# Sliding-window attention and token MLP on one core: values by four column tiles, keys in halves of 32, and a new order

## The chip, the cores and the metric

The kernel runs as one program on 1 core of one Trainium2 chip. The metric is the device time of one launch in microseconds (us); the median of several runs is compared. A core has a matrix engine (TensorE, PE in the profile, with its weight loads as PEld), a vector engine (VectorE, DVE), a scalar engine (ScalarE, ACT), a general engine (GpSimd, POOL) and a sync engine (SyncE, SP), whose queue issues nearly all DMAs here. Each engine takes its own list of instructions in order and waits on semaphores for the others. PE writes to PSUM; the others bring results from there to SBUF.

## The reference

```python
# x: [1, 2048, 512]; 32 heads of 16; window of 256 keys, causal
mod = (silu(c) @ w_mod)            # six vectors of 512: sa, ca, ga, sb, cb, gb
h = layernorm(x) * (1 + ca) + sa
q, k, v = split(h @ wqkv)          # wqkv: [512, 1536]
scores = q @ k.T * 16 ** -0.5      # kept where 0 <= query - key < 256
o = softmax(scores) @ v
x = x + ga * (o @ wo)
h = layernorm(x) * (1 + cb) + sb
u = gelu(einsum('bsd,sf->bdf', layernorm(h), w1) + b1)   # over tokens, f = 1792
y = einsum('bdf,fs->bds', u, w2) + b2
out = x + gb * y.transpose
```

All tensors are bf16.

## The kernel before

**Stages.** The 2048 tokens are cut into four row groups G of 512, each of two halves H of 256 queries. For each G the kernel normalizes x, transposes it (on PE for the first group, by DMA transposes into `h1T` for the others), and makes q, k and v with `wqkv` (`proj0` for the first group, `proj` for the rest). Then come the attention, `wo` and the next norms (`post`), and the token MLP: partial sums over finished token tiles (`partials`, pieces p), the rest of the first matmul (`tail`, pieces u), and last the output matmuls `py`, written out after the ordered part.

**Operations and their order.** All but the last stage is written as 1165 small operations (`Op`), each with an engine or a choice of engines, a cost and the operations it depends on. The list ORDER, written out in full, says in which order they are issued; CHOSEN says which engine takes each of the 177 operations that have a choice. `run_schedule` walks ORDER and emits each operation on its engine, so ORDER is the order in every engine's queue, SP's among them. The names used below are those of the operations: S (scores of a chunk, PE), EA and EB (their exponentials, ACT), M (mask, DVE), AV (values and sums, PE), ln and rz (logarithm of the sums and its exponential, ACT), OT (product, DVE), k, q, v (projections, PE), ke, qe, ve (their copies out of PSUM), kk (keys split by parity of the head), vo and vp (values placed), xn, h1T, hb, n2 (norm pieces), xt (DMA transpose), p and u (MLP, PE), wo.

**Attention in chunks.** A chunk is 512 score columns for four pairs of heads, in which four row tiles of 32 rows (two heads of 16) work at once. A column stands for one query, and the 128 partitions of a chunk hold 64 keys of each of two heads: `KT` holds, for every block of 64 keys, the keys once with the odd and once with the even heads zeroed, `[P, 8, 2, KB]`. There are 75 chunks. EA covers three of the four PSUM banks of a chunk (1536 columns), EB the fourth (512). Masks come from `maskt`, `[P, 3, KB]`, built once on POOL from triangles in `tmpm`. AV multiplies the exponentials with `VT` on four column tiles of 32, and with `ones_bd` for the sums.

**Values.** `VT[r]` has for each block of 64 keys 128 partitions, the first 64 for one head of a pair, the last 64 for the other; each half is nonzero in 16 of 32 columns. For the first group `v` makes both halves directly: two column tiles of 64, each with the 256 columns of wqkv of one parity, then a copy `vb`, and two copies multiplied with `mask_half` (all 128 partitions, 512 columns each). For the other groups `v` is a plain matmul with tokens on the partitions (four pieces of 512 columns, or sixteen in column tiles of 32). The result `vb` then has one half of the keys on the wrong partitions: `vx` swaps them by two DMAs into `vs`, `vo` copies the half that lies right, `vp` the swapped one (two copies of 64 partitions each). VT[1] is zeroed by a memset on POOL (`z`), VT[2] by two DMAs (`z2`), since these copies write the nonzero places only.

**Column tiles for dense work.** `run_schedule` marks dense PE pieces (k, q, v, wo, p) that stand near an AV in a run between two score chunks as `tiled`: `mm` then issues four matmuls of 32 output rows each instead of one of 128, so that the shape of the tiles on PE need not change.

**PSUM.** Three banks, `od`, are shared by all projections, AV, wo and p; an operation takes the bank that comes free first.

Of the kernel before, what the change touches and what calls it, by code (L numbers as in the profile page):

```python
# [13 lines left out]
P = 128  # L14
S = 2048
# [8 lines left out]
KB = 64  # L24
HQ = 4 * KB
# [91 lines left out]
]  # L117
CHOSEN = {
    "ACT": [
        47, 48, 50, 51, 74, 82, 1062,  # L120
    ],
    "DVE": [
# [5 lines left out]
    ],  # L128
    "POOL": [
# [86 lines left out]
def kernel(  # L216
# [31 lines left out]
    class Ordered:  # L248
        def __init__(self, engine):
            self.engine = engine  # L250

        def __getattr__(self, name):
            call = getattr(self.engine, name)

            def wrapped(*args, **kwargs):
                ins = call(*args, **kwargs)  # L256
                if pinned[0]:
                    tc.keep_in_program_order(ins)
# [1176 lines left out]
```

## Time and profile before

| what | us |
|---|---|
| median of 3 runs | 254.74 |
| lowest, highest | 253.11, 255.09 |
| span of the profiled execution | 252.3 |
| PE busy | 235.3 |
| DVE busy | 205.4 |
| ACT busy | 179.5 |
| POOL busy | 126.3 |

The span runs from the first to the last instruction of one profiled execution; the runs' times take in what lies around it. Busy time is the time in which an engine had at least one instruction running; since matmuls are pipelined and their ends are modelled, a busy PE is not PE at its peak. In the rows of single instructions the columns are start in us, duration in us, engine, line, operation, tile written and tiles read, shapes and count, and in brackets the idle time of the engine just before and what ended it. In the rows of groups they are count, busy us, mean ns of one, and idle us before them. Nearly every instruction has line 256, a helper through which all of them are issued, so groups are told apart by their tiles.

### The profile page before, as it was taken

What the parts mean: (1) busy time and instruction counts of PE and PEld (TensorE: products, weight loads), DVE (VectorE), ACT (ScalarE), POOL (GpSimd) and SP (SyncE); (2) the same over time, 40 slices, a digit from 0 to 9 for tenths busy, and PEclk for the clock granted to TensorE, in tenths of its full rate; (3) what the DMA queues carried; (4) which work ended last, traced back from release to release, by engine and by line L of the source; (5) the groups of instructions that cost most, each with busy time, mean ns of one, the idle gap of its engine ahead of it and who ended that gap; (6) DMA issues with size and microseconds to landing.
All of it is one profiled execution on the core that took longest, in us unless ns stands there. A gap on an engine that the chain in (4) does not pass through costs nothing.

```text
span 252.3 us, 9189 instructions
## 1 busy us (share of the span) xinstructions
PE 235.3 (93%) x3949; PEld 126.0 (50%) x3949; DVE 205.4 (81%) x408; ACT 179.5 (71%) x254; POOL 126.3 (50%) x228
## 2 busy tenths in 40 slices
PE   7988888899987889999999999999999999999995
PEld 2656644445554544555546454556444444444443
DVE  5499998989989998999897999999978764444443
ACT  4699998999999999999999999997147510000000
POOL 8268968795899989845886348173000000000000
PEclk9999999999999999999999999999999999999999
DMA  6999364356055200003401536314999201111111
GB/s 200 323 351 294 48 47 86 44 70 187 3 74 112 53 23 3 4 3 104 131 3 45 155 82 189 105 44 113 343 388 386 108 22 43 44 52 52 42 44 42
DMA packets 42625, 28.13 MB, mean 111 GB/s; under 512 B 12376, under 2 KB 38488, under 8 KB 42584
## 3 DMA queue, kind: packets, MB, share of 16 engines
q1 hardware_dynamic: 42576, 27.54, 39.4%
q8 instruction: 31, 0.51, 0.9%
q14 instruction: 10, 0.08, 0.1%
q10 hardware_dynamic: 8, 0.00, 0.0%
HBM read 22.03 MB, written 2.10 MB: 96 GB/s over the span
## 4 chain that ended last, share of the span: by engine, by line
PE 52%; ACT 24%; DVE 7%; DMA 5%; issue 5%; POOL 4%; SPq 1%; POOLq 0%; DVEq 0%
ACT et L256 20%; PE py L256 19%; PE pu L256 16%; PE po L256 5%; PE pss L256 5%; ACT lz L256 3%; PE pa L256 3%; DMA x<-in_A_x_dram 2%; DVE et L256 2%; DMA h1T<-xn 2%; DMA wmod<-in_w_mod_dram 1%; POOL h1T L256 1%; PE pq L256 1%; DVE st L256 1%; PE pk L256 1%
## 5 line engine op out<-in xcount | busy, mean ns | idle before, releaser
L256 ACT ACTIVATE et<-pss 128x1536 bf16<-128x1536 f32 x75 | 110.7, 1476 | 2.8 <-PE psb L256 2.3
L256 PE MATMUL py<-guT,w2r 128*128 128x512 bf16 (+2 forms) x238 | 48.7, 366 | 0.0
L256 ACT ACTIVATE et<-psb 128x512 bf16<-128x512 f32 x75 | 46.9, 626 | 0.0
L256 DVE TENSOR_TENSOR et<-et,maskt 128x1024 bf16<-128x1024 bf16 (+2 forms) x79 | 46.4, 603 | 0.1
L256 PE MATMUL pu<-hb,w1s 128*32 128x512 bf16 (+1 forms) x302 | 39.0, 380 | 0.2 <-DVE QT L256 0.2
L256 PEld LDWEIGHTS <-w2r 128*128 128x128 bf16 x238 | 22.8, 98 | 26.1 <-issue 0.3
L256 PE MATMUL pss<-QT,KT 32*128 32x64 bf16 (+3 forms) x720 | 29.9, 230 | 6.2 <-ACT et L256 3.5
L256 PE MATMUL po<-et,VT 128*32 128x64 bf16 (+3 forms) x960 | 32.2, 234 | 1.3 <-DVE kb L256 0.6
L256 PE MATMUL po<-et,ones_bd 128*32 128x256 bf16 (+3 forms) x624 | 31.7, 268 | 0.0
L256 PEld LDWEIGHTS <-KT 32*128 32x128 bf16 x960 | 17.1, 92 | 28.5 <-issue 24.6
L256 DVE TENSOR_TENSOR otile<-py,xr 128x512 bf16<-128x512 f32 (+2 forms) x17 | 11.2, 660 | 24.4 <-PE py L256 24.2
L256 POOL TENSOR_SCALAR KT<-kb,mask_par 128x512 bf16<-128x512 bf16 (+1 forms) x36 | 25.0, 707 | 11.4 <-DVE kb L256 11.1
L256 PE MATMUL psb<-QT,KT 32*128 32x64 bf16 (+3 forms) x240 | 29.3, 231 | 0.0
L256 PEld LDWEIGHTS <-VT 128*32 128x32 bf16 x960 | 20.8, 96 | 13.2 <-issue 4.7
L256 PE MATMUL pk<-h1T,wqkv 128*32 128x512 bf16 (+4 forms) x228 | 21.1, 340 | 2.4 <-DVE OT L256 1.0
L256 DVE BATCH_NORM_STATS2 st<-x 128x6 f32<-128x512 bf16 x32 | 21.5, 680 | 2.1 <-DMA x<-in_A_x_dram 2.1
L256 PEld LDWEIGHTS <-wqkv 128*32 128x32 bf16 (+1 forms) x350 | 15.3, 96 | 12.7 <-issue 4.7
L256 PEld LDWEIGHTS <-w1s 128*32 128x32 bf16 (+1 forms) x302 | 14.1, 97 | 15.0 <-issue 1.5
L256 PE MATMUL pv<-wqkv,h1T 128*32 128x512 bf16 (+2 forms) x202 | 17.1, 348 | 1.3 <-DVE OT L256 0.7
L256 PE MATMUL pu<-hb,w1r 128*128 128x512 bf16 (+1 forms) x96 | 17.9, 380 | 0.0
L256 PE MATMUL pa<-wod,OT 128*32 128x512 bf16 (+1 forms) x136 | 17.2, 381 | 0.0
L256 PEld LDWEIGHTS <-ones_bd 128*32 128x32 bf16 x624 | 15.8, 97 | 0.1
(109 smaller groups left out, 350.1 us busy)
## 6 DMA issues: line engine op xcount, KB each, us to landing
w2r<-in_B_w_dram SPq DMA_DIRECT2D x14, 512.0 KB, 10.2
w1s<-in_B_w_dram SPq DMA_DIRECT2D x19, 256.0 KB, 4.0
w1r<-in_B_w_dram SPq DMA_DIRECT2D x9, 256.0 KB, 4.3
x<-in_A_x_dram SPq DMA_DIRECT2D x16, 128.0 KB, 5.2
wmod<-in_w_mod_dram SPq DMA_DIRECT2D x4, 512.0 KB, 7.8
out_dram<-otile SPq DMA_DIRECT2D x15, 128.0 KB, 1.7
wmod<-in_w_mod_dram SPq DMA_DIRECT2D x4, 256.0 KB, 3.9
wqkv<-in_A_wqkv_dram SPq DMA_DIRECT2D x4, 256.0 KB, 5.7
```

The costliest lines, as they stand in the source:

```text
L256: ins = call(*args, **kwargs)
```

## The change

Five things change; the number of operations and the names stay.

1. The values of all groups are made like this, for each half n of a token tile, with four column tiles of 32 partitions (32 tokens each, one parity of the heads each). They then lie on the right partitions, and are placed by two masked copies over all 128 partitions, as in the first group before. The swaps and both zero fills go; their operations stay in the list as empty ones.
2. The partitions of a chunk change their order: 32 keys of one head, the same 32 of the other, then the next 32 of each. `KT`, `mask_half`, `ones_bd` and `maskt` follow.
3. Pieces in units of 32 columns allow new shapes of chunks (`NEAR_MIXED`, `FAR_MIXED`, one chunk of 256 columns for both), used for the first MIXED pairs; MIXED is 0. `maskt` has ten parts instead of three, for these shapes too.
4. `v` counts as a neighbour that makes dense pieces `tiled`, the first group's too, which had a class of its own before. `vb` has three buffers instead of two.
5. ORDER and CHOSEN are new lists; each instruction also gets an explicit dependency, without a semaphore, on the one before it on its engine.

```diff
+QB = 32
...
-        sums = [n for n, o in enumerate(run) if o.name == "AV"]
+        sums = [n for n, o in enumerate(run) if o.name == "AV" or o.name == "v"]
...
-NEAR = [(-1, 0, 4, 0), (0, 0, 4, 256)]
+MIXED = 0
+NEAR = [(-1, 0, 8, 0), (0, 0, 8, 256)]
...
+                    if self.last is not None:
+                        tc.add_manual_dep(
+                            ins.ins, self.last, mybir.DependencyInfo(mybir.DependencyClass.NoSync, mybir.DependencyReason.DATA),
+                            reason="order",
+                        )
+                    self.last = ins.ins.name
...
-    KT = [[kvpool.tile([P, 8, 2, KB], BF, name=f"KT{r}_{g}") for g in range(ND)] for r in range(3)]
+    KT = [[kvpool.tile([P, 8, 2, 2, QB], BF, name=f"KT{r}_{g}") for g in range(ND)] for r in range(3)]
...
-        1: [op("z", "POOL", 3.45, lambda e: po.memset(VT[1][:], 0.0), ready=2.0, pos=-22.0)],
+        1: [op("z", "POOL", 0.05, lambda e: None, pos=-22.0)],
...
+    def values(dst, h1T, tb, n):
+        wv = wqkv[:, :, 2 * D : 3 * D].rearrange("p j (a two d) -> p j two a d", two=2, d=DH)
+        for dc in range(ND):
+            for r in range(4):
+                tok = tb * P + n * KB + r // 2 * QB
+                te.matmul(
+                    dst[QB * r : QB * (r + 1), n, :].rearrange("p (a d) -> p a d", d=DH),
+                    lhsT=h1T[:, dc, tok : tok + QB], rhs=wv[:, dc, r % 2, :, :],
+                    start=(dc == 0), stop=(dc == ND - 1), tile_position=(0, QB * r), skip_group_check=True,
+                )
+
+    def place(eng, dst, src, tb, half):
+        eng.tensor_scalar(
+            out=dst[:, 2 * tb : 2 * tb + 2, :, half * DH : (half + 1) * DH],
+            in0=src[:].rearrange("p i (a d) -> p i a d", d=DH),
+            scalar1=mask_half[:, half : half + 1], scalar2=0.0, op0=ALU.mult, op1=ALU.add,
+        )
...
-            zeros[2].append(op("z2", "SP", 2.6, lambda e, n=n: dma.dma_start(
-                out=VT[2][:, 4 * n : 4 * n + 4, :, :].rearrange("p b a d -> p b (a d)"),
-                in_=nothing[:].unsqueeze(1).to_broadcast([P, 4, D]),
-            ), deps=zeros[2] + k_done[0, 1][-1:], pos=14.0 + n, ready=30.0, extra=1.0))
+            zeros[2].append(op("z2", "SP", 0.0, lambda e: None, deps=zeros[2] + k_done[0, 1][-1:], pos=14.0 + n, extra=-2.0))
...
-            def e_vx(e):
-                vs = box["vs", tb] = work.tile([P, 256], BF, name="vs", tag=vs_tag, bufs=1)
-                dma.dma_start(out=vs[0:KB, :], in_=box["vb", tb][KB:P, 0, :])
-                dma.dma_start(out=vs[KB:P, :], in_=box["vb", tb][0:KB, 1, :])
...
-            vx = op("vx", "SP", 1.05, e_vx, deps=[ve_op], pos=pos, extra=0.1)
-            own = op("vo", {"POOL": 0.78, "DVE": 0.45}, 0.78, lambda e: e_vp(e, True), deps=[ve_op] + war + zeros[r3], pos=pos)
-            b = op("vp", {"POOL": 0.78, "DVE": 0.45}, 0.78, lambda e: e_vp(e, False), deps=[vx] + war + zeros[r3], pos=pos)
+            vx = op("vx", "SP", 0.0, lambda e: None, deps=[ve_op], pos=pos, extra=-2.0)
+            placed = [
+                op(("vo", "vp")[half], {"POOL": 0.78, "DVE": 0.45}, 0.78,
+                   lambda e, half=half: place(ENGINE[e], VT[r3], box["vb", tb], tb, half), deps=[ve_op] + war, pos=pos)
+                for half in range(2)
+            ]
```

In CHOSEN the changes by name, engine before and after, are: m2 four from DVE to POOL and four back; n2 four to POOL, two to DVE; hb four to POOL, one to DVE; xn three to POOL, one to DVE; kk three to DVE, one to POOL; vo two each way; vp two to DVE; h1T two from DVE to POOL, one from POOL to DVE, one from ACT to DVE; ke one from ACT to DVE; ve one from DVE to ACT.

More of the change, by code (lines that the diff above doesn't have):

```diff
@@ L250, in __init__ @@
             self.engine = engine
+            self.last = None
         def __getattr__(self, name):
@@ L300 @@
     wod = const.tile([P, ND, D], BF, name="wod")
-    maskt = const.tile([P, 3, KB], BF, name="maskt")
+    maskt = const.tile([P, 10, QB], BF, name="maskt")
     ones_bd = const.tile([P, 2 * DH], BF, name="ones_bd")
     nc.gpsimd.memset(ones_bd[:], 0.0)
-    nc.gpsimd.memset(ones_bd[0:KB, 0:DH], ZSCALE)
-    nc.gpsimd.memset(ones_bd[KB:P, DH : 2 * DH], ZSCALE)
+    for r in range(4):
+        nc.gpsimd.memset(ones_bd[QB * r : QB * (r + 1), r % 2 * DH : (r % 2 + 1) * DH], ZSCALE)
     nothing = const.tile([P, D], BF, name="nothing")
@@ L380, in emit_masks @@
     def emit_masks():
-        tmpm = modw.tile([P, 2, 2, KB], BF, name="tmpm")
+        tmpm = modw.tile([P, 3, 2, KB], BF, name="tmpm")
+        masks = maskt[:].rearrange("p m k -> p (m k)")
         po.memset(tmpm[:], 1.0)
-        for half in range(2):
+        for n in range(3):
             po.affine_select(
-                out=tmpm[:, half, 0, :], in_=tmpm[:, half, 0, :], pattern=[[-1, KB]],
-                compare_op=ALU.is_ge, fill=0.0, base=-1 - KB * half, channel_multiplier=1,
+                out=tmpm[:, n, 0, :], in_=tmpm[:, n, 0, :], pattern=[[-1, KB]],
+                compare_op=ALU.is_ge, fill=0.0, base=-1 - QB * n, channel_multiplier=1,
             )
             po.affine_select(
-                out=tmpm[:, half, 1, :], in_=tmpm[:, half, 1, :], pattern=[[1, KB]],
-                compare_op=ALU.is_ge, fill=0.0, base=KB * half, channel_multiplier=-1,
-            )
-        for half in range(2):
-            rows = slice(KB * half, KB * half + KB)
-            for i in range(3):
-                po.tensor_copy(out=maskt[rows, i, :], in_=tmpm[rows, half, min(i, 1), :])
+                out=tmpm[:, n, 1, :], in_=tmpm[:, n, 1, :], pattern=[[1, KB]],
+                compare_op=ALU.is_ge, fill=0.0, base=QB * n, channel_multiplier=-1,
+            )
+        for r, n in enumerate((0, 1, 1, 2)):
+            rows = slice(QB * r, QB * (r + 1))
+            both = tmpm[rows, n, :, :].rearrange("p s k -> p (s k)")
+            parts = both.rearrange("p (n k) -> p n k", k=QB)
+            po.tensor_copy(out=masks[rows, 0:128], in_=both)
+            po.tensor_copy(out=masks[rows, 128:192].rearrange("p (n k) -> p n k", k=QB), in_=parts[:, 0:4:3, :])
+            for to, part in ((192, 1), (256, 2)):
+                po.tensor_copy(
+                    out=masks[rows, to : to + KB].rearrange("p (n k) -> p n k", k=QB),
+                    in_=parts[:, part : part + 1, :].to_broadcast([QB, 2, QB]),
+                )
     ops = []
@@ L812, in e_v @@
                     box["v", tb] = bank([P, 2, 256], F32, "pv")
-                wv = wqkv[:, :, 2 * D : 3 * D].rearrange("p j (a two d) -> p j two a d", two=2, d=DH)
-                tok = slice(tb * P + n * KB, tb * P + (n + 1) * KB)
-                for dc in range(ND):
-                    for par in range(2):
-                        te.matmul(
-                            box["v", tb][KB * par : KB * (par + 1), n, :].rearrange("p (a d) -> p a d", d=DH),
-                            lhsT=h1T[:, dc, tok], rhs=wv[:, dc, par, :, :],
-                            start=(dc == 0), stop=(dc == ND - 1), tile_position=(0, KB * par),
-                        )
+                values(box["v", tb], h1T, tb, n)
             def e_ve(e):
@@ L974, in e_v @@
                 if n == 0:
-                    box["v", tb] = bank([P, D], F32, "pv")
-                for dc in (2 * n, 2 * n + 1):
-                    mm(
-                        box["v", tb][:], h1T[:, dc, tb * P : (tb + 1) * P], wqkv[:, dc, 2 * D : 3 * D],
-                        (dc == 0), (dc == ND - 1),
-                    )
-            def e_ve(e):
-                vb = box["vb", tb] = work.tile([P, 2, 256], BF, name="vb", tag=vb_tag, bufs=1)
-                copy(
-                    e, vb[:].rearrange("p two (a d) -> p a two d", d=DH),
-                    box["v", tb][:].rearrange("p (a two d) -> p a two d", two=2, d=DH),
-                )
-            def e_vx(e):
-                vs = box["vs", tb] = work.tile([P, 256], BF, name="vs", tag=vs_tag, bufs=1)
-                dma.dma_start(out=vs[0:KB, :], in_=box["vb", tb][KB:P, 0, :])
-                dma.dma_start(out=vs[KB:P, :], in_=box["vb", tb][0:KB, 1, :])
-            def e_vp(e, own):
-                for half in range(2):
-                    rows = slice(KB * half, KB * half + KB)
-                    block, src = (half, box["vb", tb][rows, half, :]) if own else (1 - half, box["vs", tb][rows, :])
-                    ENGINE[e].tensor_copy(
-                        out=VT[r3][rows, 2 * tb + block, :, half * DH : (half + 1) * DH],
-                        in_=src.rearrange("p (a d) -> p a d", d=DH),
-                    )
-            vb_tag, vs_tag = turn("vb"), turn("vs")
+                    box["v", tb] = bank([P, 2, 256], F32, "pv")
+                values(box["v", tb], h1T, tb, n)
+            def e_ve(e):
+                box["vb", tb] = work.tile([P, 2, 256], BF, name="vb", tag=vb_tag, bufs=1)
+                copy(e, box["vb", tb][:], box["v", tb][:])
+            vb_tag = turn("vb", 3)
             war = [av_ops[G - 2, g] for g in range(ND)] if G >= 2 else []
@@ L1168, in e_s, with score @@
                 box["sb", i] = ps_b.tile([P, D], F32, name="psb")
-                for unit, kb, qs, nq, col in pieces:
-                    g8, Hh = unit["g8"], unit["H"]
-                    block = 4 * Hh + kb
-                    q0 = (Hh % 2) * HQ + KB * qs
+                def score(unit, kb, q, width, col, side=None):
+                    block = 4 * unit["H"] + kb
+                    own = KT[block // 8 % 3][unit["g8"]]
+                    q += (unit["H"] % 2) * HQ
+                    part = slice(0, P) if side is None else slice(KB * side, KB * (side + 1))
                     for j in range(4):
                         rows = slice(32 * j, 32 * j + 32)
-                        dst = box["sa"][:, j, col : col + KB * nq] if j < 3 else box["sb", i][:, col : col + KB * nq]
+                        dst = box["sa"][part, j, col : col + width] if j < 3 else box["sb", i][part, col : col + width]
                         te.matmul(
-                            dst, lhsT=KT[block // 8 % 3][g8][rows, block % 8, :, :],
-                            rhs=QT[unit["G"] % 2][g8][rows, q0 : q0 + KB * nq],
-                            start=True, stop=True, tile_position=(32 * j, 0), skip_group_check=True,
-                        )
+                            dst, lhsT=own[rows, block % 8, :, :, :] if side is None else own[rows, block % 8, side, :, :],
+                            rhs=QT[unit["G"] % 2][unit["g8"]][rows, q : q + width],
+                            start=True, stop=True, tile_position=(32 * j, part.start), skip_group_check=True,
+                        )
+                for unit, kb, qs, nq, col in pieces:
+                    if kb is not None:
+                        score(unit, kb, QB * qs, QB * nq, col)
+                    else:
+                        for qb in range(4):
+                            for side in range(2):
+                                score(unit, qb - 4 * side, KB * qb + QB * side, QB, col + QB * qb, side)
             def e_ea(e, i=i, lo=lo, hi=hi):
```

112 lines of the change are left out of this document (69 added, 43 removed), and 123 rows, old and new, of tables (CHOSEN, ORDER).

## The prediction

> **What bounds the kernel now.** I read the page first, then the engines' busy time in six stretches, then the chain of waits, then single rows. The page's totals and its slices come first:
>
> ```profile
> span 252.3 us, 9189 instructions
> PE 235.3 (93%) x3949; PEld 126.0 (50%) x3949; DVE 205.4 (81%) x408; ACT 179.5 (71%) x254; POOL 126.3 (50%) x228
> PE   7988888899987889999999999999999999999995
> ACT  4699998999999999999999999997147510000000
> ```
>
> By shares PE is the bound and ACT is at 71%. The slices say otherwise: ACT is full from the third slice to the twenty-eighth and then nearly idle. So I cut the span where the second exponential starts (14.58), where PE becomes full (115), just behind the last score chunk (171) and at the first output matmul (200.94). Columns: PE, weight loads, DVE, ACT, POOL.
>
> ```profile
> 14.58:115.00 100.42, 89.74 (x2126) 51.91 (x2128) 94.99 (x189) 98.92 (x134) 82.78 (x140) 1.00 0.38 81
> 115.00:171.00 56.00, 55.32 (x1228) 30.13 (x1224) 51.97 (x96) 55.40 (x74) 33.42 (x59) 1.00 0.35 97
> 171.00:200.94 29.94, 29.94 (x257) 14.57 (x246) 26.19 (x61) 15.06 (x30) 1.73 (x2) 1.00 0.80 281
> 200.94:252.30 51.36, 48.55 (x239) 22.57 (x236) 24.09 (x39) 1.70 (x3) 0.00 (x0) 1.00 0.12 42
> ```
>
> From 14.58 to 171 ACT is busy 154.3 of 156.4 us: the exponentials set the pace, and DVE, at 147, has little room either. PE has 10.7 us of room up to 115 and none after. Behind the last score chunk PE alone counts, without a gap:
>
> ```profile
> 169.87 0.26 PE L256 MATMUL pss<-QT,KT 32*128 32x192 bf16 x3
> 178.50 22.45 PE pu L256 x104
> 203.78 45.75 PE py L256 x225
> ```
>
> So the time is: start of the exponentials, plus ACT's work and ACT's stalls up to the last score chunk, plus the PE work left behind it. Only the middle term has slack, and little. The group row sums ACT's stalls, and three single rows show what one is:
>
> ```profile
> L256 ACT ACTIVATE et<-pss 128x1536 bf16<-128x1536 f32 x75 | 110.7, 1476 | 2.8 <-PE psb L256 2.3
> 11.22 1.45 ACT L256 ACTIVATE et<-pss 128x1536 bf16<-128x1536 f32 x1 [0.73 <-PE psb L256]
> 40.47 1.45 ACT L256 ACTIVATE et<-pss 128x1536 bf16<-128x1536 f32 x1 [0.64 <-PE psb L256]
> 83.05 1.45 ACT L256 ACTIVATE et<-pss 128x1536 bf16<-128x1536 f32 x1 [0.42 <-PE psb L256]
> ```
>
> In each the score matmuls came late from PE. All 75 exponentials together stood 2.8 us, 0.73 of it before the first one; the other 2.1 us is all that a better order can take out of the middle term.
>
> **The change, part by part.** *The work behind the last score chunk.* I walked both ORDER lists to the last S entry. Behind it the old list has 56 u, 4 p, 4 wo and 7 AV, the new one the same with 6 AV. The AV that moves ahead of it (two times 512 columns, at 22.45 / 104 = 0.216 us each: 0.43) lands where PE is full as well, so I count nothing. MIXED is 0, so no chunk takes the new mixed shapes: 75 chunks with the old column counts, and ACT's exponentials stay as they are.
>
> *Values on PE.* A token tile was 4 matmuls of 512 columns on the whole array (or 16 in column tiles), in the first group 16 of 256 columns on two tiles; it becomes 32 of 256 columns on four. The trace has that count and shape for keys:
>
> ```profile
> 28.69 1.06 PE L256 MATMUL pk<-h1T,wqkv 128*32 128x256 bf16 x32 [0.39 <-DVE bc_ga L256]
> 14.47 1.06 PE L256 MATMUL pv<-wqkv,h1T 128*64 128x256 bf16 x16
> L256 PE MATMUL pv<-wqkv,h1T 128*128 128x512 bf16 x18 | 4.7, 380 | 0.6 <-DVE vb L256 0.6
> ```
>
> 32 such matmuls took 1.06 us, as the two-tile form did, against 4.7 / 4.5 = 1.04 us for a tile of the whole-array form. Cost of the new form: nothing. Walking the lists, the tile shape on PE changes 153 times instead of 158: nothing I can price above a few tenths, and up to 115 under ACT's cover.
>
> *Placing the values.* Four copies of half the partitions become two masked copies of all; the zero fills go.
>
> ```profile
> L256 POOL COPY VT<-vs 64x256 bf16<-64x256 bf16 x24 | 10.8, 452 | 3.9 <-DMA vs<-vb 3.0
> L256 POOL COPY VT<-vb 64x256 bf16<-64x256 bf16 x20 | 10.2, 511 | 3.5 <-DVE vb L256 2.9
> L256 DVE COPY VT<-vb 64x256 bf16<-64x256 bf16 x4 | 0.9, 216 | 0.0
> L256 POOL TENSOR_SCALAR VT<-vb,mask_half 128x512 bf16<-128x512 bf16 x8 | 5.8, 731 | 1.3 <-DVE vb L256 1.3
> L256 POOL MEMSET VT<- 128x4096 bf16 x1 | 3.5, 3517 | 0.1
> L256 DVE TENSOR_SCALAR KT<-kb,mask_par 128x512 bf16<-128x512 bf16 x2 | 1.0, 526 | 0.0
> ```
>
> By CHOSEN 20 of the 24 new copies are on POOL: 20 x 0.731 = 14.6 against 10.8 + 10.2 + 3.5 = 24.5 us, so POOL gains 9.9. Four are on DVE, priced at the like key copy: 4 x 0.526 = 2.1 against 0.9, so DVE pays 1.2.
>
> [...]
>
> *Masks.* POOL builds them from six selects instead of four and sixteen copies instead of six:
>
> ```profile
> L256 POOL COPY maskt<-tmpm 64x64 bf16<-64x64 bf16 x6 | 1.2, 234 | 0.0
> L256 POOL TENSOR_SCALAR_AFFINE_SELECT tmpm<-tmpm 128x64 bf16<-128x64 bf16 x4 | 0.9, 268 | 0.1
> 13.15 3.03 POOL L256 TENSOR_SCALAR KT<-kb,mask_par 128x256 bf16<-128x256 bf16 x6 [5.19 <-DVE kb L256]
> 11.75 0.69 DVE L256 BATCH_NORM_STATS2 st<-x 128x6 f32<-128x512 bf16 x1 [1.02 <-DMA x<-in_A_x_dram]
> ```
>
> 10 x 0.234 + 2 x 0.268 = 2.9 us more, less the 3.5 of the memset ahead of them: they end no later, and POOL then stood idle 5.19 us anyway. Without that cover the first key copies would be late.
>
> The last row also fixes the start. The second chunk's keys wait on DVE for statistics of an x tile that lands at 11.75, and both lists have those statistics ahead of the key copy. So the second exponential stays near 14.58, although one h1T piece goes from ACT to DVE before it.
>
> *ACT's own list.* One key copy leaves it, one value copy (512 columns) enters behind the third exponential:
>
> ```profile
> 14.26 0.37 ACT L256 ACTIVATE kb<-pk 128x256 bf16<-128x256 f32 x1
> 14.58 1.45 ACT L256 ACTIVATE et<-pss 128x1536 bf16<-128x1536 f32 x1
> 15.93 0.59 ACT L256 ACTIVATE et<-psb 128x512 bf16<-128x512 f32 x1
> ```
>
> The 0.37 lay before 14.58 and saves nothing. The entering copy, at the 0.59 of a 512-column piece, which overlaps its neighbour by 0.1, costs +0.5 us, with every exponential queued behind it.
>
> *SP's queue.* 24 swaps and two fills go from it:
>
> ```profile
> vs<-vb SPq DMA_DIRECT2D x24, 32.0 KB, 1.9
> VT<-nothing SPq DMA_DIRECT2D x2, 512.0 KB, 4.7
> SPq L256 <- DVE vb L256: 55.3, 6, 23.4
> ```
>
> SP stood 55.3 us waiting for vb, with transposes and w1 loads queued behind. That makes inputs early, not PE late: in no row above did PE or ACT wait for a swap or a load, so I take nothing; the bound on the other side is ACT's 2 us.
>
> *The order.* The second h1T piece of group 1 goes from POOL to DVE, so the two run side by side:
>
> ```profile
> 39.70 0.40 PE L256 MATMUL pk<-h1T,wqkv 128*32 128x512 bf16 x4 [0.70 <-POOL h1T L256]
> L256 POOL TENSOR_SCALAR h1T<-h1T,modFM 128x512 bf16<-128x512 bf16 x8 | 7.2, 907 | 2.4 <-DMA h1T<-xn 2.3
> L256 DVE TENSOR_SCALAR h1T<-h1T,modFM 128x512 bf16<-128x512 bf16 x4 | 1.5, 426 | 0.0
> ```
>
> The pair ends up to 2 x 0.907 us earlier, which takes away the 0.70 wait and with it the 0.64 stall of ACT at 40.47. Next late there are the DVE copies of k and q. Net of all moves POOL takes three hb, two n2, two xn and one h1T, and DVE two key splits:
>
> ```profile
> L256 POOL TENSOR_SCALAR hb<-h,rs,nm 128x512 bf16<-128x512 bf16 x8 | 6.7, 844 | 0.4
> L256 DVE TENSOR_SCALAR hb<-h,rs,nm 128x512 bf16<-128x512 bf16 x4 | 2.5, 627 | 0.0
> ```
>
> At the hb price the seven norm pieces take 7 x 0.627 = 4.4 us off DVE and put 5.9 on POOL; the two key splits give DVE back 4 x 0.526 = 2.1, the placing 1.2. The single pieces exchanged with ACT about cancel. DVE ends 1.1 us lighter of 147, so its room grows by an eighth (1.1 of 9.4), and I take an eighth, 0.2, off the remaining 1.4 us of stalls.
>
> **Sum.** +0.5 (value copy on ACT) - 0.64 (h1T stall) - 0.2 (DVE) = -0.3 us on the profiled span of 252.3: 252.0. The runs lie 0.8 to 2.8 us above the span, their median 254.74 is 2.4 above; with the same 2.4 I forecast **254.4**. Own range of this case: from 252.4 (nearly every stall gone) to 257.2 (the new order stalls 2.8 us more, as much as the old one in all).
>
> **Rivals.** *All stalls go* (chance 0.17). The 2.1 us and the 0.73 before the first exponential vanish and the value copy finds a hole: 254.74 - 2.83 = 251.9, and 251.5 if the AV's 0.43 counts as well. For it: SP and POOL lose real work. Against: the stalls named above come from DVE and from PE's own queue, which the change barely touches.
>
> *Scores behind a late piece* (0.23). PE takes its list in order; every score chunk stands behind dense pieces whose inputs the new list places anew. If such an input is late, ACT stands. One event costs 0.42 to 0.64 (the two rows above). The place is the joints of the row groups, about 38 to 41 and 65 to 86 us, where the seven norm pieces now sit on POOL, 5.9 us in front of key splits and value copies. It decides from about five events more than now, 2.9 us; with nine, 5.4. That gives 257.3 to 259.8, say 258.3. For it: ACT has 2.1 us of idle time in 156, so a new order has more to lose than to win.
>
> *Four strided streams* (0.08). The value matmuls stream wqkv in runs of 16 of every 32 columns, now four streams at a time; the 28.69 row streams plain columns on four tiles, the 14.47 row strided ones on two. If reading limits, a tile takes twice its 2048 columns, 4 x 0.216 = 0.86 us more. By the new list three of the 16 tiles stand behind 115, where PE is full: +2.6; the 13 before them cost 11.2 against PE's 10.7 of room: 257 at the least, 268 if none is hidden. Against: at two streams the strided row took the same 1.06 us as the plain one.
>
> [...]
>
> *Does it do what it says?* The fills and swaps leave SP, but where SP's next entry waits for its own input (11 of the 12 transposes follow an xn on POOL in the new list) nothing comes earlier; that is inside the forecast.
>
> **Chances and range.** Forecast 0.52, nearly all of it within 1% (252.2 to 257.3, about what a measurement of this kernel can tell from no change); stalls gone 0.17; late pieces 0.23, nearly all beyond 1%; strided streams 0.08. Faster by over 1%: 0.17 + 0.02 from the forecast's lower edge = 0.19; slower: 0.23 + 0.08 + 0.01 = 0.32; within: 0.49. Eight in ten: 251.4 to 258.8, from the end of the first rival to the middle of the second's upper half.
>
> **What would show it.** Right: the second exponential near 14.6, the last score chunk near 169.5, no idle PE behind it, a value tile at about 1.06 us, no stall at the first k of group 1. Wrong: the last score chunk beyond 172 with ACT idle behind PE (late pieces), or value tiles near 1.9 us (streams); a start of the second exponential well before 14.3, or less PE work behind the last score chunk, would break the sum itself.

## The result and the profile after

The changed kernel took 256.66 us (median of 4 runs, 256.43 to 256.78); the kernel before, in runs beside it, 254.09 (4 runs, 253.11 to 255.09). The ratio is 1.0115, with a 95% interval from 1.0075 to 1.0155. The forecast was 254.4: the time lies in its range, but the kernel became slower by a little more than 1%, and the forecast was no change. In some executions the granted clock is lower and the time longer (of the kernel before, 256.69 us at 0.987 and 252.75 at 1.000); below, medians are of all runs, while the ratios leave out those more than 1.5% above the fastest of their kernel.

The page of the changed kernel, with the lines that answer to those of before (here nearly every instruction has line 259, and line numbers differ a little between the experiments too):

```profile
span 254.8 us, 9881 instructions
...
PE 234.9 (92%) x4331; PEld 131.6 (52%) x4331; DVE 207.1 (81%) x404; ACT 179.3 (70%) x253; POOL 128.5 (50%) x224
...
ACT  4699998999998799999999999999226620000000
...
L259 ACT ACTIVATE et<-pss 128x1536 bf16<-128x1536 f32 x75 | 110.2, 1470 | 5.6 <-PE psb L259 4.8
```

ACT was busy 179.3 us instead of 179.5, PE 234.9 instead of 235.3; DVE has 1.7 and POOL 2.2 more, less than 2% each. What doubled is the idle time in the last line: the time ACT stood before its exponentials, 5.6 us where it was 2.8. In the slices the full stretch of ACT has two new dents, at the thirteenth and the fourteenth (the seventh was at 8 before too). The busy time by stretches (columns: PE, weight loads, DVE, ACT, POOL) says the same:

```profile
14.58:115.00 100.42, 87.61 (x2331) 55.09 (x2323) 92.59 (x179) 95.47 (x128) 82.30 (x124) 1.00 0.34 74
115.00:171.00 56.00, 54.32 (x1306) 30.54 (x1294) 53.31 (x95) 55.32 (x75) 33.49 (x49) 1.00 0.30 82
```

Up to 115 us ACT did 95.47 us of work where it had done 98.92, and PE and DVE lost about 2 us each with it: all three wait. Behind the last score chunk nothing was lost:

```profile
173.33 0.26 PE L259 MATMUL pss<-QT,KT 32*128 32x192 bf16 x3
...
203.66 48.55 PE L259 MATMUL py<-guT,w2r 128*128 128x512 bf16 x238
```

From 173.33 to the end of the span are 81.5 us; before, from 169.87, it was 82.4. So the loss came ahead of the last chunk. The starts of single exponentials in both timelines show where (chunks counted from 0; us after the change less us before):

| chunk | 1 | 2 | 12 | 16 | 29 | 42 | 66 | 74 |
|---|---|---|---|---|---|---|---|---|
| start after | 13.99 | 15.94 | 37.66 | 47.68 | 74.66 | 105.86 | 155.86 | 173.77 |
| later by | -0.59 | -0.59 | 0.04 | 1.04 | 0.71 | 3.54 | 2.51 | 3.46 |

The start is better than before. About 0.6 us goes up to chunk 12, 1.0 at the joint of the first two row groups (38 to 47 us), and 2.8 between chunks 29 and 42, most of it at the next joint, 75 to 92 us; 1.0 comes back up to chunk 66, and 0.9 goes again behind it. The stretch from chunk 29 to chunk 42, 31.20 us here and 28.37 before, is the measure for the second joint below. What stands there in the timeline of the changed kernel (start, duration, engine, instruction, idle time before it and what ended it):

```profile
71.64 0.77 POOL L259 TENSOR_SCALAR xn<-x,rs,nm 128x512 bf16<-128x512 bf16 x1
...
73.15 0.93 POOL L259 TENSOR_SCALAR xn<-x,rs,nm 128x512 bf16<-128x512 bf16 x1
74.07 1.45 POOL L259 TENSOR_SCALAR h<-x,rs,nm 128x512 bf16<-128x512 bf16 x1
75.50 1.52 POOL L259 TENSOR_SCALAR KT<-kb,mask_par 128x512 bf16<-128x512 bf16 x2
77.00 3.01 POOL L259 TENSOR_SCALAR VT<-vb,mask_half 128x512 bf16<-128x512 bf16 x3
...
80.04 0.69 DVE L259 CAST vb<-pv 128x512 bf16<-128x512 f32 x1 [0.59 <-POOL VT L259]
...
80.78 0.40 PE L259 MATMUL po<-et,VT 128*32 128x256 bf16 x8 [1.48 <-DVE vb L259]
...
82.29 1.38 DVE L259 TENSOR_TENSOR h<-h,bc_cb 128x512 bf16<-128x512 bf16 x1
...
84.89 0.29 PE L259 MATMUL po<-et,VT 128*32 128x128 bf16 x8 [1.51 <-DVE OT L259]
...
86.10 1.45 ACT L259 ACTIVATE et<-pss 128x1536 bf16<-128x1536 f32 x1 [1.41 <-PE psb L259]
```

Read it from the top. POOL works without a gap, first through norm pieces, then through the split of the keys, then through three value copies, which end at 80.01. All three vb buffers are in use, and the first is free when the last of these copies is done. So DVE's copy of the next value tile out of PSUM (in this profile DVE makes 15 of the 16 such copies and ACT one; POOL reads no PSUM tile here or in the profile of before) stands at the head of DVE's queue until 80.04, with everything on DVE behind it. The tile's PSUM bank is one of the three that AV shares: PE stands 1.48 us. It stands again, 1.51 us, some 4 us later, because DVE brings OT late: two norm pieces stand ahead of OT in DVE's queue, and the first took 1.38 us at 82.29, where its mean had been 0.448 before. The next scores stand behind this on PE, and ACT waits 1.41 us. The kernel before, on POOL in the same stretch:

```profile
70.01 1.52 POOL L256 TENSOR_SCALAR KT<-kb,mask_par 128x512 bf16<-128x512 bf16 x2
71.52 0.79 POOL L256 TENSOR_SCALAR xn<-x,rs,nm 128x512 bf16<-128x512 bf16 x1
...
74.07 0.93 POOL L256 TENSOR_SCALAR xn<-x,rs,nm 128x512 bf16<-128x512 bf16 x1
...
76.13 1.40 POOL L256 COPY VT<-vb 64x256 bf16<-64x256 bf16 x2
```

The same kinds of pieces, but the key split came first, at 70.01 instead of 75.50. (It is operation 326, the last key split of row group 1, counted from 0; DVE's next key copy, at 77.05, waited 0.59 us for its input buffer.) The new list also issues the first three value tiles of row group 2 close together: with chunks 26, 27 and 28, where the old list had 27, 29 and 33.

### The profile page after: what moved, and what is told of

The parts are those of the page before. It is cut to its first block, busy times and chain, and to the rows that moved or that the text cites. A ratio compares the mean times of both kernels' runs of the same rounds, so it can differ in the third digit from the quotient of the medians.

```text
span 254.8 us, 9881 instructions
## 1 busy us (share of the span) xinstructions
PE 234.9 (92%) x4331; PEld 131.6 (52%) x4331; DVE 207.1 (81%) x404; ACT 179.3 (70%) x253; POOL 128.5 (50%) x224
## 4 chain that ended last, share of the span: by engine, by line
PE 48%; DVE 13%; POOL 13%; ACT 12%; issue 7%; DMA 4%; SPq 2%; POOLq 0%; DVEq 0%
PE py L259 19%; PE pu L259 15%; ACT et L259 10%; PE po L259 4%; PE pss L259 3%; DVE st L259 3%; DVE et L259 3%; ACT lz L259 2%; DVE h L259 2%; PE pa L259 2%; DMA x<-in_A_x_dram 2%; POOL sq L259 2%; POOL VT L259 2%; POOL rs L259 2%; DMA h1T<-xn 2%
## 5 line engine op out<-in xcount | busy, mean ns | idle before, releaser
L259 PE MATMUL pu<-hb,w1s 128*32 128x512 bf16 (+1 forms) x272 | 38.3, 381 | 0.7 <-DVE OT L259 0.7
L259 PE MATMUL pss<-QT,KT 32*128 32x64 bf16 (+3 forms) x720 | 30.3, 230 | 7.6 <-ACT et L259 5.1
L259 PE MATMUL po<-et,VT 128*32 128x64 bf16 (+3 forms) x960 | 32.3, 234 | 4.3 <-DVE OT L259 1.5
L259 POOL TENSOR_SCALAR VT<-vb,mask_half 128x512 bf16<-128x512 bf16 x28 | 23.8, 858 | 10.8 <-DVE vb L259 9.8
L259 PEld LDWEIGHTS <-VT 128*32 128x32 bf16 x960 | 21.7, 96 | 12.0 <-issue 6.1
L259 POOL TENSOR_SCALAR KT<-kb,mask_par 128x512 bf16<-128x512 bf16 (+1 forms) x32 | 22.7, 721 | 5.9 <-DVE kb L259 5.8
L259 PE MATMUL pv<-wqkv,h1T 128*32 128x256 bf16 x512 | 17.4, 273 | 1.5 <-POOL h1T L259 1.4
L259 PE MATMUL pu<-hb,w1r 128*32 128x512 bf16 (+1 forms) x120 | 17.6, 379 | 0.0
L259 PE MATMUL pa<-wod,OT 128*32 128x512 bf16 (+1 forms) x118 | 16.5, 381 | 0.0
## 6 DMA issues: line engine op xcount, KB each, us to landing
w1s<-in_B_w_dram SPq DMA_DIRECT2D x19, 256.0 KB, 4.0
w1r<-in_B_w_dram SPq DMA_DIRECT2D x9, 256.0 KB, 3.7
wmod<-in_w_mod_dram SPq DMA_DIRECT2D x4, 256.0 KB, 3.5
wqkv<-in_A_wqkv_dram SPq DMA_DIRECT2D x4, 256.0 KB, 5.1
```

## The experiments

**The new form with the old lists, and the new ORDER with the old CHOSEN.** Since form and lists changed together, I first took them apart (the long lists are named here, not printed).

```diff
-ORDER and CHOSEN of the changed kernel
+ORDER and CHOSEN of the kernel before
```

> All of the new code with the ORDER and CHOSEN of before. If the loss sits in the new lists: 253.3 to 254.5 us (before: 254.1), ACT stalls about 2 to 3 us in all, as before. If it sits in the new form (masked copies on POOL, 32-row column tiles): 256 to 257, with the stalls of the changed kernel (5.6 us).

Measured: 253.51 us (10 runs), ratio 0.9991 [0.9967, 1.0015]. Its page:

```profile
span 251.4 us, 9818 instructions
...
L262 ACT ACTIVATE et<-pss 128x1536 bf16<-128x1536 f32 x75 | 110.7, 1476 | 2.4 <-PE psb L262 1.9
```

So values on four column tiles, masked copies, halves of 32 keys, the larger masks and the explicit dependencies together can't be told from the old form, and with the old lists ACT's waits are those of before. The loss comes with the new lists.

```diff
 ORDER of the changed kernel
-CHOSEN of the changed kernel
+CHOSEN of the kernel before
```

> The changed kernel with the CHOSEN of before, so that seven norm pieces go back from POOL to DVE; ORDER stays new. If POOL is late because it was given too much: 254.3 to 255.4 and a shorter PE wait near 81 us. If the places in the queues are the cause, not the engines: 256.2 to 257.2. If the form is the cause: 256.7.

Measured: 281.97 us (4 runs), ratio 1.1014 [1.0936, 1.1092]. No expectation came near it. ORDER and CHOSEN can't be judged one without the other: on engines for which it was not made, the order makes PE stand for 3 us at several places. The first of them, and the stretches around it:

```profile
29.01 1.06 PE L260 MATMUL pv<-wqkv,h1T 128*32 128x256 bf16 x32 [3.07 <-DVE vb L260]
```

```profile
24.00:26.00 2.00, 1.94 (x80) 1.58 (x73) 0.72 (x2) 2.00 (x3) 1.79 (x6) 1.00 0.34 102
26.00:28.00 2.00, 0.00 (x0) 0.00 (x0) 0.06 (x1) 2.00 (x4) 1.63 (x4) 1.00 0.03 8
28.00:30.00 2.00, 0.99 (x32) 0.77 (x32) 2.00 (x5) 0.29 (x1) 1.98 (x3) 1.00 0.01 4
30.00:32.00 2.00, 0.41 (x20) 0.32 (x17) 2.00 (x6) 1.55 (x2) 2.00 (x3) 0.65 0.55 112
32.00:34.00 2.00, 1.57 (x40) 1.40 (x43) 2.00 (x7) 0.39 (x1) 1.57 (x3) 0.50 0.42 85
```

The third number from the end of a row is PE's granted clock: after the gap it falls to 0.50. Twelve value matmuls of 64 columns, with PE then at 0.50, took 0.62 us at 32.42, where the like took 0.41 at 32.15 in the changed kernel, at 1.00. The mean granted clock of this execution was 0.957 over 280.9 us, which by estimate is worth 12 us of full speed at most (0.043 x 280.9); the waits on PE make up the rest of the 28 us. The run says nothing on the 2.6 us of the change.

**One suspect at a time.** Three kernels each took one link out of what I had seen: two norm pieces, the number of vb buffers, and, at the first joint, the norm piece ahead of the transposes.

```diff
+def move(n, ahead_of):
+    ORDER.remove(n)
+    ORDER.insert(ORDER.index(ahead_of), n)
...
+move(728, 247)
+move(734, 247)
```

> The changed kernel with two norm pieces of the last row group (xn, not needed for 20 us more) moved behind the value copies in POOL's queue. If the joint at 75 to 86 us is late because POOL reaches its value copies late: POOL reaches them 1.9 us earlier, the PE wait of 1.48 before 80.78 falls below 0.5, ACT's stalls there by 1 to 1.5, and the time is 255.2 to 255.8. If DVE's own queue holds that joint: 256.4 to 256.9.

Measured: 257.47 us (4 runs), ratio 1.0100 [1.0042, 1.0159]. In its trace the wait of 1.48 us is down to 0.28, the stall at 86 us is gone, and chunks 29 to 42 took 29.03 us instead of 31.20; but the moved pieces now stand in front of another key split:

```profile
88.80 0.28 PE L276 MATMUL pss<-QT,KT 32*128 32x256 bf16 x3 [1.19 <-POOL KT L276]
89.14 1.45 ACT L276 ACTIVATE et<-pss 128x1536 bf16<-128x1536 f32 x1 [1.07 <-PE psb L276]
```

By the trace the place is right, and the move puts the pieces ahead of the next piece that is waited for. The median can't tell what the move is worth: the traced execution, 255.02, was the fastest of the four, and the others took 257.46 to 259.61. In this trace DVE's norm piece took its short time, and PE had no wait for OT:

```profile
80.50 0.41 DVE L276 TENSOR_TENSOR h<-h,bc_cb 128x512 bf16<-128x512 bf16 x1
```

```diff
-turn("vb", 3)
+turn("vb", 4)
```

> The changed kernel with four buffers for vb instead of three, so that DVE's value copy at 80.04 need not wait 0.59 us for POOL to finish with an older one. If that wait is the link between POOL and PE: the joint comes 0.6 us earlier or more, 255.7 to 256.3. If POOL's lateness reaches PE another way: 256.5 to 256.9.

Measured: 256.14 us (6 runs), ratio 1.0083 [1.0056, 1.0109]. The buffer halves the first wait and leaves the second (chunks 29 to 42: 30.52 us):

```profile
79.87 0.40 PE L259 MATMUL po<-et,VT 128*32 128x256 bf16 x8 [0.74 <-DVE vb L259]
84.06 0.30 PE L259 MATMUL po<-et,VT 128*32 128x128 bf16 x8 [1.59 <-DVE OT L259]
```

So the vb buffers are a link of the chain, but not its beginning.

```diff
+move(273, 105)
```

(a norm piece of the first transposes, ahead of a value copy on POOL)

> The changed kernel with one norm piece (xn of the last tile of group 1) moved ahead of two value copies and a key split in POOL's queue. If the joint at 41 us is late because that tile's transpose waits for POOL: the transposes land about 2.6 us earlier, the PE wait of 1.42 before 38.93 and ACT's stall of 1.27 at 41.23 go, and all later exponentials start about 1 us earlier: 255.4 to 256.0. If DMA itself or DVE sets that joint: 256.4 to 256.9.

Measured: 256.96 us (4 runs), ratio 1.0121 [1.0077, 1.0165]. The stall at 41 us is gone from its trace, whose execution took 255.87, the fastest of the four, and the median is no better. Nor is it shown that the move did it: the last of the four transposes was issued at 32.5 us, as in the changed kernel, and only landed earlier. A miss for the first joint.

**All three together.**

```diff
-turn("vb", 3)
+turn("vb", 4)
...
+move(273, 105)
+move(728, 730)
+move(734, 730)
```

(the two norm pieces now stand only just behind the key split and value copies, ahead of the next of their kind)

> The changed kernel with that piece ahead, the two norm pieces of the last group behind one key split more than in the run with two pieces moved (so that no key split waits for them), and four vb buffers. If the loss is the sum of late pieces at two joints: ACT's stalls come back to 2 to 3 us in all and the time to 253.6 to 254.8, level with before. If something else in the new lists costs as much: 255.3 to 256.5.

Measured: 254.31 us (12 runs), ratio 1.0031 [1.0003, 1.0059]: nearly the whole loss is back.

**Two smaller suspects.** The value copy that the new CHOSEN gives to ACT, back on DVE; and the explicit dependencies left out.

```diff
+engine(91, "DVE")
```

(`engine` moves an operation, here the value copy, to another engine's list in CHOSEN)

> The changed kernel with the one value copy on ACT back on DVE. By the prediction's sum every exponential behind it starts 0.4 to 0.5 us earlier and the span is 254.3. If the joint at 41 us is set by POOL and DMA alone, the gain ends there: the exponential at 41.23 starts within 0.15 of that, and the span is 254.6 to 255.0.

Measured, one run: 258.26, a span of 256.6, above both expectations. The copy gone, the exponential of chunk 3 comes 0.36 us earlier behind that of chunk 2, but an ACT stall of 0.54 at 22.5 us takes that and more back. The 0.5 us that I had put on this copy doesn't show as a gain in this run.

```diff
-                    if self.last is not None:
-                        tc.add_manual_dep(...)
-                    self.last = ins.ins.name
```

> The changed kernel without the explicit dependency of each instruction on the one before it. If it only fixes an order that the list gives already: the same instructions in the same order and a span of 254.4 to 255.2. If it costs waits: a span below 254.

Measured, one run: 255.64, a span of 253.8. That is just below the 254 named for a dependency that costs waits; but one run can't tell that from an execution that happens to lack the stall at 41 us. Every engine's instructions have the same order as in the changed kernel. From 75 us on the stalls are those of the changed kernel within 0.1 us; the one at 41 us is missing. POOL's start of h1T in the changed kernel and here:

```profile
37.23 1.70 POOL L259 TENSOR_SCALAR h1T<-h1T,modFM 128x512 bf16<-128x512 bf16 x2 [1.95 <-DMA h1T<-xn]
```

```profile
35.00 1.95 POOL L259 TENSOR_SCALAR h1T<-h1T,modFM 128x512 bf16<-128x512 bf16 x2 [0.34 <-DMA h1T<-xn]
```

The four DMA transposes that it waits for were issued from 27.26 us in the one and from 27.09 in the other, the last at 32.5 and 32.3, and landed 2 us apart. This gave a second theory, "landing": the loss is the late transposes of the first joint.

**The two joints against each other, and the mirror.** Four kernels, compared with the same 29 runs of the kernel before (254.04 us).

> The changed kernel once more, as the yardstick of this group, and a second profile of it. Theory "bunched joint" (most of the loss sits in the stretch from 75 to 90 us, where norm pieces on GpSimd stand ahead of key splits and value copies): 256.4 to 256.9 again; the stalls of ScalarE at about 77, 82, 86, 93 and 101 us come back in this profile within 0.2 us of their size. Theory "landing" (the loss is the late DMA transposes at 41 us): the stall at 41 us decides the time; an execution without it is near 255.2, so the times spread from 255 to 257. For both the 41 us stall itself can come out anywhere from 0 to 1.3 us.

The changed kernel unedited: 257.27 us (6 runs), ratio 1.0134 [1.0105, 1.0164]. The stalls come back at 77.8 (0.48), 82.5 (0.59), 86.5 (1.40) and 102.8 us (0.54), the one at 93 us (0.41) does not; the one at 41 us is 0.98 this time. Behind the two long waits on PE (1.42 and 1.50 us) the granted clock was 0.50 here for a while, which the first profile of this kernel doesn't have:

```profile
84.00:86.80 2.80, 1.35 (x40) 0.88 (x43) 2.77 (x6) 1.40 (x4) 2.80 (x4) 1.00 0.00 0
87.00:90.00 3.00, 3.00 (x56) 1.48 (x46) 3.00 (x7) 2.04 (x4) 3.00 (x5) 0.50 0.67 49
```

```diff
-turn("vb", 3)
+turn("vb", 4)
...
+move(728, 730)
+move(734, 730)
```

> Only the two moves at the second joint (two norm pieces behind the key split and the value copies on GpSimd) and a fourth vb buffer, with the first joint left as the change has it. Theory "bunched joint": 254.2 to 255.2, the wait of 1.48 us for vb and the ScalarE stall of 1.41 gone or under 1.1; if the stall at 41 us is there in the profile, the time is at the upper end. Theory "landing": 256.0 to 256.7, as the run with the four buffers alone.

Measured: 254.35 us (12 runs), ratio 1.0027 [1.0003, 1.0051], with the first joint as the change has it. Its timeline:

```profile
71.30 2.28 POOL L276 TENSOR_SCALAR h<-x,rs,nm 128x512 bf16<-128x512 bf16 x3
73.56 2.21 POOL L276 TENSOR_SCALAR KT<-kb,mask_par 128x512 bf16<-128x512 bf16 x2
75.74 2.19 POOL L276 TENSOR_SCALAR VT<-vb,mask_half 128x512 bf16<-128x512 bf16 x3
...
79.73 0.40 PE L276 MATMUL po<-et,VT 128*32 128x256 bf16 x8 [0.29 <-DVE vb L276]
...
81.23 1.38 DVE L276 TENSOR_TENSOR h<-h,bc_cb 128x512 bf16<-128x512 bf16 x1
...
83.83 0.30 PE L276 MATMUL po<-et,VT 128*32 128x128 bf16 x8 [1.28 <-DVE OT L276]
...
85.04 1.45 ACT L276 ACTIVATE et<-pss 128x1536 bf16<-128x1536 f32 x1 [1.03 <-PE psb L276]
```

The key split starts at 73.56 instead of 75.50, the wait for vb is 0.29 instead of 1.48, the ACT stall 1.03 instead of 1.41. Chunks 29 to 42 took 28.95 us, against 31.20 in the changed kernel and 28.37 before. What stays is the wait for OT, 1.28 us, so POOL's value copies made little of it: DVE's norm piece again took 1.38 us. By the medians 2.9 of the 3.2 us between the kernel before and the changed one in this group (257.27 - 254.35, of 257.27 - 254.04) are gone, although this profile had the largest stall of all at 41 us (1.75). "Landing" had expected 256.0 at the least. It is out as the main cause; with the transposes' piece moved as well (254.31 above) the median is the same.

```diff
-ORDER and CHOSEN of the changed kernel
+ORDER and CHOSEN of the kernel before
+for n in (732, 245, 247, 734):
+    move(n, 326)
+for n in (527, 528, 529):
+    move(n, 519)
```

> The mirror: the new form with the old lists, which took 253.5 us, and at the second joint alone the new list's bunch put in: four norm pieces on GpSimd ahead of the first key split of row group 2, and the second value tile straight behind the first two. Theory "bunched joint": 255.0 to 256.5, with new ScalarE stalls of 1 to 2 us between 76 and 90 us. Theory "landing", and any theory by which the rest of the new list is what costs: 253.3 to 254.0.

Measured: 254.86 us (10 runs), ratio 1.0038 [1.0012, 1.0064]. By the ratios (1.0038 and 0.9991, in another group of runs) the bunch alone costs the old lists about 1.2 us, and by the traces 1.27, in the place expected: chunks 29 to 42 took 29.67 us, and 28.40 with the plain old lists.

```profile
76.12 1.45 ACT L281 ACTIVATE et<-pss 128x1536 bf16<-128x1536 f32 x1 [1.15 <-PE psb L281]
...
76.40 3.11 DVE L281 TENSOR_TENSOR et<-et,maskt 128x1024 bf16<-128x1024 bf16 x2
...
80.16 0.40 PE L281 MATMUL po<-et,VT 128*32 128x256 bf16 x8 [1.83 <-DVE kb L281]
...
81.60 1.45 ACT L281 ACTIVATE et<-pss 128x1536 bf16<-128x1536 f32 x1 [0.99 <-PE psb L281]
```

It lies just under the expected 255.0 to 256.5 and above the other theories' 254.0. Moving norm pieces and a value tile at once, it doesn't say which of the two costs how much. Part of it isn't the waiting for POOL either: the two masks at 76.40 took 3.11 us on DVE, where one took 0.742 on the mean before, while POOL ran two pieces of two inputs each (76.25 to 78.96). The joint is enough to make a loss, and a little less than half of the size.

```diff
-ORDER and CHOSEN of the changed kernel
+ORDER and CHOSEN of the kernel before
+move(527, 528)
```

> Candidate to beat both: the new form with the old lists, and one half of a value tile moved behind the score chunk that waited for it (ScalarE stall of 0.53 us at 82.4). If stalls are what the time is made of, as both theories say: 252.9 to 253.3 against 253.5 without the move, and the stall gone. If the later vector engine work takes it back: 253.4 to 253.8.

Measured: 253.18 us (12 runs), ratio 0.9990 [0.9969, 1.0011]. The chunk that had stalled 0.53 us comes 0.7 earlier, and the next one gives it all back:

```profile
84.68 1.45 ACT L278 ACTIVATE et<-pss 128x1536 bf16<-128x1536 f32 x1 [0.68 <-PE psb L278]
```

Neither this kernel nor the one with the plain old lists can be told from the kernel before. No version here beats it.

**Both joints in the traces.** The time between the exponentials of two chunks, in us, in one profiled execution each:

| kernel | chunks 12 to 16 | chunks 29 to 42 |
|---|---|---|
| before | 9.02 | 28.37 |
| changed | 10.02 | 31.20 |
| changed, second profile | 9.64 | 32.07 |
| changed, no explicit dependencies | 8.61 | 31.11 |
| fourth buffer alone | 8.92 | 30.52 |
| two norm pieces moved, three buffers | 9.61 | 29.03 |
| moved pieces and fourth buffer | 10.50 | 28.95 |
| all three together | 8.62 | 28.94 |
| new form, old lists | 8.60 | 28.40 |
| the same with the bunch | 8.25 | 29.67 |

The second joint follows the order of the lists: the moved norm pieces take most of its loss away. The first joint swings by nearly 2 us, also with one and the same order of all engines (10.02 and 8.61), as the transposes land.

## Why the prediction was wrong

**The step that failed** is the term "ACT's stalls" of the sum, worked out under "The order". I took the 2.1 us of stalls of the old list over to the new one, as if a new list could only lessen them, and subtracted 0.64 for the h1T pair and 0.2 for a lighter DVE. But stalls belong to a list. The new one made its own: 5.6 us by the row of the exponentials where I had 2.0 left. That is inside the own range of my forecast (its upper end was "the new order stalls 2.8 us more"), but I put the forecast itself below the old kernel without a reason from the new list. The 0.2 rested on a DVE that would be 1.1 us lighter; it came out 1.7 heavier (207.1 for 205.4). The step from span to runs was off as well: I added 2.4 us, from the median of other executions, but every run here lies 1.7 to 1.9 us above its own span, by which the same sum gives 253.8.

**The rival "scores behind a late piece" is what happened**, at the places it named, by the pieces it named: norm pieces on POOL in front of key splits and value copies. The move of two of them with a fourth buffer brings 2.9 us back by the medians (2.25 of 2.83 in the stretch of the traces), and the mirror makes a loss in the old lists. I gave it 0.23. Its size was put too high (258.3 for 256.7): the priced 0.42 to 0.64 an event fits most of them (0.49, 0.41, 0.38, 0.63), two were larger (1.41, and 1.27 at 41 us), and I counted on more. Two links I had not seen. One is the buffer: a value copy that is late on POOL holds vb, and so DVE's whole queue and a PSUM bank, which makes a stall out of lateness. The other is a norm piece on DVE that is long beside one on POOL: the largest stall, 1.41, stood behind a DVE piece of 1.38 us, and was missing in the trace where that took 0.41. No run tests this link alone.

It could have been read beforehand. I summed POOL's and DVE's loads over all 154 us, where POOL has room. Between `nm` and the key split 326 the new list has five norm pieces on POOL, three h and two xn, and the old list none; at the 0.91 and 0.93 us that these had on POOL in the profile of before this makes 4.6 us, and the key split did come 5.5 us later (75.50 for 70.01; `nm` itself came 0.75 later).

**The joint at 41 us.** The forecast was that the h1T pair, split over two engines, would end earlier and the stall of 0.64 go. It was 1.27 in the profile of the changed kernel, from 0.3 to 1.75 in five other profiles with the same list at that place, and 0 in one: both halves of the pair start together now, as forecast, but when the transposes land. The step was right for the engines and overlooked that a DMA releases them (its own row said so: 2.3 of the 2.4 us before h1T on POOL).

**Values on PE cost nothing**: right. The rival "four strided streams" is out.

```profile
L259 PE MATMUL pv<-wqkv,h1T 128*32 128x256 bf16 x512 | 17.4, 273 | 1.5 <-POOL h1T L259 1.4
L259 POOL TENSOR_SCALAR VT<-vb,mask_half 128x512 bf16<-128x512 bf16 x28 | 23.8, 858 | 10.8 <-DVE vb L259 9.8 <-ACT vb L259 0.9
L259 DVE TENSOR_TENSOR h<-h,bc_cb 128x512 bf16<-128x512 bf16 x12 | 7.2, 604 | 0.2 <-POOL h L259 0.2
L259 DVE TENSOR_SCALAR VT<-vb,mask_half 128x512 bf16<-128x512 bf16 x4 | 1.8, 459 | 0.0
```

A matmul took 273 ns, as those of before did; sixteen tiles at 17.4 us are 1.09 each, against the 1.06 in the forecast. **Placing**: on POOL a copy took 0.858 us, not 0.731 (the row of before was from the first group alone), so POOL's 28 copies took 23.8 us where copies and fill had been 30.3 (10.8, 10.2, 5.8 and 3.5): 6.5 us given back instead of 9.9. On DVE a copy took 0.459, below the 0.526 of the row it was priced at. Neither sets the time, as the run with the old lists shows. **SP's freed queue, masks, tile shapes**: nothing, by the same run; I took them at nothing.

**The value copy on ACT** was to cost 0.5. It delays the exponential next to it by 0.36, but in the one run without it the time was no better; so it seems hidden in the end.

**The start**: second exponential at 13.99 where I had 14.6. The start varies between the executions here (13.99 to 14.73 for the list of the changed kernel), so a few tenths of this are no effect of the order. **The work behind the last chunk**: 81.5 instead of 82.4. The forecast took the AV that moved ahead as worth nothing, because PE is full there. Its 0.43 would be half of the difference, if PE had room for it before the last chunk (54.32 us busy of the 56 up to 171, where it was 55.32); no run tests this, and the other half is not explained.

Of the signs that were to tell right from wrong, the one for late pieces came true to the letter: the last score chunk at 173.33, beyond 172, with ACT idle behind PE. The two that were to break the sum itself came too, a start before 14.3 (13.99) and less work behind the last chunk (by 0.9); both made the kernel faster, and from the second exponential to the last score chunk it took about 4 us more.

**Open.** About 0.5 to 1 us stays between the mended list and the old one with the new form (254.35 and 253.51, in different groups). The stalls left in the mended one's profile are the 1.03 at 85 us, behind DVE's OT, and 0.63 at 157 us; no run removes them. With the last places of the two norm pieces, the fourth buffer was not left out. How often an unprofiled execution has the stall at 41 us is not known either, so it stays open how much of the 2.9 us between the medians is luck at the first joint; the traces show 2.25 for the second.

## What to carry to other kernels

Where an order of all engines is written out by hand, its stalls don't carry over to a new order: price each order by itself, stretch by stretch. Take the slowest in-order engine ahead of each due piece, add up what the list puts before that piece in the stretch, and ask which buffer, PSUM bank and queue is held until it is done. A busy share over the whole span hides such a bunch: POOL stood at 50%, and most of the loss began in its queue. Look also at what DVE runs at the same time: here one of its norm pieces took three times its mean beside one of POOL's (1.38 us, and 0.448 on the mean before).

## What was not expected of the hardware

- **Gaps on PE went ahead of a halved clock, and not only long ones.** With the new ORDER on the old engines PE stood 3.07 us before 29.01, and the granted clock fell from 1.00 to 0.50 a little later. In the first profile of the changed kernel no PE wait in these joints was over 1.51 us and the clock stayed at 1.00; in its second profile the longest was 1.50 us, and the clock was 0.50 from 87 to 90 us. Over the 2.80 us from 84.00 PE was busy 1.72 us in the first and 1.35 in the second. No run here shows what sets the fall.
- **Transposes issued at the same time landed up to 2 us apart** from one execution to another: POOL's h1T started at 35.00 us in one and at 37.23 in another, with the same instructions in the same order on all engines.
- **The same DVE operation took 0.45 or 1.38 us.** Combining two tiles on DVE (h with bc_cb) had a mean of 0.448 us before; at 82.29 us, where POOL ran an operation of two inputs (82.17, 1.22 us), it took 1.38. With the fourth buffer and the moved pieces it took 1.38 again, beside the same operation of POOL (81.11, 1.22 us). Beside POOL's operations it was not always that long: 0.80 at 79.80 in the profile of before, beside the same operation of POOL (79.17, 1.15 us), and 0.41 at 80.50 with two norm pieces moved, beside one with a single tile as input (80.27, 1.20 us). That POOL is the cause is not shown.
